# Moving the small product that turns the mu rows, in a retention and channel-mix kernel

## The chip, the cores and the metric

The kernel runs on one core of a Trainium2 chip. The metric is device time in microseconds (us) of one execution. PE is the matrix engine (TensorE) and PEld its weight loads, DVE the vector engine, ACT the scalar engine, POOL the engine that issues most input transfers, SP the one that issues the stores. An engine works through its own instructions in the order in which they were written, and waits at the first one whose inputs are not ready.

## What is computed

Two layers, one behind the other. The first is a linear attention with a decay gamma for each head (batch 4, 8 heads, 768 tokens, 64 features a head):

```python
for t in range(S):
    state = gamma * state + einsum('bhd,bhe->bhde', k[:, :, t], v[:, :, t])
    y[:, :, t] = scale * einsum('bhd,bhde->bhe', q[:, :, t], state)
x = y.transpose(0, 2, 1, 3).reshape(B, S, 512)
```

The second mixes each token with the one before it, by two vectors `mu_k` and `mu_r` of 512 numbers, and applies three weight matrices:

```python
xk = mu_k * x + (1 - mu_k) * x_prev
xr = mu_r * x + (1 - mu_r) * x_prev
k = maximum(xk @ w_k, 0)          # 512 -> 1024
v = k * k @ w_v                   # 1024 -> 512
out = sigmoid(xr @ w_r) * v
```

## The kernel before

The tokens are cut into 12 blocks of 256 (three for each batch entry). For a block, the attention runs in its chunked form. PE turns q and k (codes `Tq`, `Tk`, L272), ACT copies the turned halves out of PSUM (`Eq`, `Ek`, L241), PE makes the scores (`S`, L339 in block 0, L331 in blocks 1 to 5), DVE masks them (`M`, L354), DVE scales v (`vs`, L253), PE makes the block's addition to the state (`C`, L395 in block 0, L384 in block 1), DVE or ACT adds it up (`U`, L419 and L241), ACT applies the decay for the next block (`G`, L424), PE makes the output from masked scores and v (`Y`, L489 in block 0, L478 in block 1) and from the carried state (`I`, `J`, L441), and DVE writes it as x, token features across partitions (`D`, L514). `Y` of block 0 takes in the second part of the state's product too.

The second layer takes the difference of neighbouring tokens (`dx`, L529), mixes it with mu (`X`, L538), and runs the products `K` (L552, L562), `R` (L592) and `V` (L604), with Relu and Square on ACT (`Qa`, `Qb`), Sigmoid (`s`), the last multiplication on DVE (`O`, L610) and the store (`st`).

What sets the order is a string written out by hand, `ORDER` (L23 to L74). Each word is one step: a code, the block and further indices, `~` with an engine and `@` with the PSUM banks that it uses. L719 walks through the string and issues each step's instructions; so a word's place sets the place of its instructions in the queue of each engine. The scheduler adds semaphore waits where data or a PSUM bank demand them, and moves nothing.

Block 0 is done in two halves of the head pairs (`0.2` and `2.4` at the end of a word). Its first halves of q and k come through SP into a staging tile and are cast by ACT (`cq`, `ck`); the second halves come through POOL. Words `z.N` are products of a tile of zeros, N quarters of an fp32 product each (L667), or fp16 products for what is left of N by four (L674). Nobody reads their results.

The vectors mu come in as eight rows of 128 numbers: the word `mu` (L652) issues two transfers of 2 KB from ACT's queue. The word `mt` (`trans_mu`, L658) turns the eight rows on PE into eight columns, in PSUM bank 3. The word `me` (`copy_mu`, L661) copies these from PSUM to the tile `mu` on ACT. The first reader of that tile is the first `X` of block 0 on DVE. Behind `me` on ACT stand `gy.1` (L685, the upper half of a table of gamma powers, four instructions) and `G.0` (L424, four instructions).

Input tiles for q, k and v are rings of four, and POOL's transfers also take turns on eight completion semaphores: an issue waits for the one eight before it to land.

Of the kernel before, what the change touches and what calls it, by code (L numbers as in the profile page):

```python
# [20 lines left out]
WIDE = (1, 2, 3, 4, 5)  # L21
HEADS = ((0, 1), (3, 2), (4, 5), (7, 6))
ORDER = """  # L23
lk.0.0.2~s gy.0 lq.0.2.4~p lv.0~p lq.0.0.2~s lk.0.2.4~p ck.0.0.2~a z.12@6 Tk.0.0.2@0 mu Tq.0.2.4@1
cq.0.0.2~a z.2@6 Tq.0.0.2@2 Ek.0.0.2~a vs.0~v mt@3 Eq.0.0.2~a z.2@6 S.0.1.0.2@45 S.0.0.0.2@67
M.0.0.0.2~v Eq.0.2.4~a M.0.1.0.2~v Tk.0.2.4@2 Ek.0.2.4~a C.0@01 U.0.0~a U.0.1 S.0.0.2.4@67
M.0.0.2.4~v I.0@45 S.0.1.2.4@01 me M.0.1.2.4~v lv.1~p vs.1~v gy.1~a G.0~a z.4@2 Y.0 D.0~v lk.1~p
Tk.1@0 Ek.1~a C.1@67 U.1.0 lq.1~p z.1@2 Tq.1@1 Eq.1~a dx.0~v X.0.0.0 z.4@2 S.1.1@01 lk.2~p I.1@45
S.1.0@23 M.1.1~v M.1.0~v lq.2~p Tq.2@6 Eq.2~a wk.1~p X.0.0.3 Tk.2@0 X.0.0.2 z.1@1 Y.1 J.1 X.0.0.1
D.1~v U.1.1 Ek.2~a z.1@2 S.2.1@01 S.2.0@23 K.0.2@6 dx.1~v K.0.3@4 Qa.0.3 Qa.0.2 wk.0~p z.2@5  # L30
K.0.1@7 Qa.0.1 K.0.0@5 Qb.0.2 X.0.1.0 X.1.0.2 lv.2~p Qa.0.0 Qb.0.1 X.1.0.3 wr~p X.1.0.1 X.1.0.0
K.1.2@4 lv.3~p G.1~a K.1.1@7 X.0.1.1 vs.2~v Qa.1.2 Qb.1.2 M.2.1~v Qb.0.0 C.2@5 U.2.0 K.1.0@6
lq.3~p Qa.1.1 X.0.1.2 X.0.1.3 K.1.3@0 Qa.1.3 I.2@45 R.0.1@1 R.0.0@7 s.0.1 M.2.0~v Y.2 Qa.1.0
X.1.1.3 X.1.1.2 Qb.1.0 Tq.3@1 Eq.3~a J.2 X.1.1.0 X.1.1.1 R.1.0@6 s.0.0 lk.3~p Tk.3@1 vs.3~v D.2~v
dx.2~v X.2.0.2 X.2.0.0 C.3@23 X.2.0.3 Ek.3~a s.1.0 X.2.0.1 lk.4~p U.3.0~a R.1.1@0 lq.4~p s.1.1
Tk.4@1 S.3.1@45 S.3.0@67 Qb.1.1 Qb.1.3 U.3.1 lv.4~p Tq.4@0 Ek.4~a Eq.4~a wv.0~p K.2.2@2 Qa.2.2
M.3.1~v K.2.0@3 Qa.2.0 G.3~a M.3.0~v K.2.3@1 vs.4~v Qb.0.3 S.4.1@45 S.4.0@67 M.4.0~v I.3@23
M.4.1~v Qa.2.3 lq.6~p lq.7~p K.2.1@0 Qb.2.0 Y.3 C.4@67 V.1.0.0@1 U.4.0 U.4.1 G.4~a I.4@45 J.3
Qa.2.1 D.3~v dx.3~v Y.4 V.1.1.0@6 Tq.7@23 J.4 D.4~v wv.1~p Qb.2.1 V.0.1.0@0 lk.6~p V.0.0.0@7
X.2.1.2 dx.4~v X.3.0.1 X.3.0.2 X.3.0.3 Eq.7~a V.1.1.1 X.3.0.0 V.0.0.1 O.0.0 Tk.6@45 Ek.6~a lq.5~p  # L40
Tq.6@23 lv.5~p Qb.2.2 V.0.1.1 Eq.6~a V.1.0.1 O.1.0 K.3.6@4 K.3.1@5 Qb.2.3 lk.5~p K.3.0@7 Qa.3.6
Tq.5@4 Qa.3.1 Qa.3.0 vs.5~v C.5@5 X.2.1.1 Eq.5~a Tk.5@1 Ek.5~a S.6@23 O.0.1 O.1.1 lk.7~p U.5.0
Tk.7@67 Ek.7~a X.2.1.0 I.5@45 M.6~v X.3.1.3 K.3.2@0 K.3.3@1 Qa.3.2 Qb.3.1 lv.6~p S.5.0@23 Qa.3.3
Qb.3.0 X.3.1.1 S.5.1@67 Qb.3.3 X.2.1.3 Qb.3.2 K.3.4@0 st.0.0 Qa.3.4 M.5.1~v lk.8~p K.3.5@1 Qa.3.5
R.2.1@6 lv.8~p lk.9~p s.2.1 M.5.0~v Y.5 S.7@23 Tk.8@01 Ek.8~a J.5 X.3.1.0 X.3.1.2 R.3.1@7 s.3.1
V.2.0.0@6 K.3.7@0 lv.7~p vs.6~v R.2.0@7 V.2.0.1 D.5~v M.7~v s.2.0 dx.5~v X.5.1.1 O.2.0 Qa.3.7
Qb.3.6 V.2.1.0@1 Tk.9@23 C.6@45 U.6.0~a Ek.9~a lq.8~p Tq.8@67 Qb.3.7 X.5.0.3 V.2.1.1 vs.7~v
R.4.0@0 Eq.8~a U.6.1 U.6.2 X.5.0.0 U.6.3 st.0.1 R.3.0@2 C.7@45 X.5.0.1 s.4.0 I.6@67 s.3.0 st.1.1
X.5.0.2 K.5.3@3 Qa.5.3 O.2.1 lq.10~p K.5.1@0 Qa.5.1 G.6~v X.5.1.3 V.3.0.0@1 U.7.0 U.7.1 U.7.2
st.2.1 I.7@23 Y.6 vs.8~v U.7.3 G.7~a lq.11~p R.4.1@0 D.6~v V.4.1.0@4 lv.11~p C.8@67 Y.7 V.3.1.0@5  # L50
Qb.5.1 Qb.3.4 Qb.3.5 V.3.0.1 dx.6~v s.4.1 U.8.0 U.8.1 V.3.1.1 Qb.5.3 D.7~v U.8.2 V.4.1.1 dx.7~v
X.6.0.1 X.6.0.3 V.4.0.0@7 K.5.0@6 X.5.1.2 X.6.0.2 Qa.5.0 V.4.0.1 Qb.5.0 K.5.2@0 X.6.0.0 Qa.5.2
Qb.5.2 X.6.1.2 lv.9~p K.6.7@6 Qa.6.7 st.2.0 st.1.0 O.4.1 O.3.0 K.6.0@2 Qa.6.0 lk.10~p O.4.0 O.3.1
st.3.1 K.6.4@0 S.8@67 I.8@23 Tk.10@45 Qa.6.4 K.6.1@1 Ek.10~a X.6.1.1 X.5.1.0 Qa.6.1 Qb.6.1 K.6.6@0
Qb.6.0 Qa.6.6 vs.9~v K.6.5@4 Qa.6.5 M.8~v R.5.1@1 Qb.6.6 Tq.10@67 Eq.10~a s.5.1 Y.8 Tq.11@45
Qb.6.7 lv.10~p vs.10~v X.6.1.3 Eq.11~a D.8~v dx.8~v lq.9~p X.8.0.2 X.8.0.1 lk.11~p R.5.0@0 s.5.0
K.6.3@6 Qa.6.3 V.5.1.0@7 Tq.9@23 X.6.1.0 Eq.9~a S.10@45 M.10~v Qb.6.3 C.9@01 U.9.0~v st.3.0 U.9.1
V.5.1.1 K.6.2@6 Qa.6.2 R.6.1@2 s.6.1 U.9.2 R.6.0@3 s.6.0 I.9@45 U.9.3 O.5.1 X.8.0.3 S.9@01 M.9~v
X.8.0.0 G.9~a C.10@67 U.10.0 U.10.1 Qb.6.2 vs.11~v R.7.1@2 s.7.1 V.5.0.0@3 Qb.6.5 st.4.1 Tk.11@01
Ek.11~a U.10.2 U.10.3 V.5.0.1 Qb.6.4 K.8.0@2 Qa.8.0 G.10~v I.10@01 Y.9 C.11@67 st.4.0 R.7.0@2  # L60
O.5.0 V.6.1.0@3 D.9~v U.11.0 U.11.1 s.7.0 K.8.3@4 Qa.8.3 V.6.1.1 U.11.2 I.11@67 st.5.0 dx.9~v
O.6.1 S.11@45 X.8.1.2 Y.10 V.7.1.0@2 M.11~v D.10~v dx.10~v X.9.0.3 X.9.0.2 X.9.0.1 V.7.0.0@3 Y.11
X.9.0.0 Qb.8.0 K.8.2@4 Qa.8.2 X.8.1.0 X.9.1.1 K.8.1@5 Qa.8.1 D.11~v V.6.0.0@0 V.7.0.1 V.6.0.1
K.9.3@1 K.9.7@5 Qa.9.7 X.8.1.1 V.7.1.1 X.8.1.3 dx.11~v K.9.2@4 O.7.0 Qb.8.1 Qb.9.7 O.6.0 Qa.9.3
st.5.1 Qa.9.2 X.11.1.0 Qb.8.3 X.11.0.3 K.9.1@5 K.9.4@6 st.7.0 Qa.9.1 Qb.9.1 R.8.0@1 s.8.0
V.8.1.0@3 Qb.9.2 X.9.1.0 K.9.0@0 Qa.9.0 Qb.8.2 X.9.1.2 Qb.9.3 K.9.6@1 Qa.9.6 Qb.9.6 O.7.1 st.7.1
K.9.5@7 Qa.9.5 V.8.0.0@0 X.11.0.2 X.11.0.1 Qb.9.0 X.11.0.0 K.11.3@2 K.11.0@1 Qa.11.3 st.6.1
R.8.1@5 V.8.1.1 X.11.1.2 Qa.9.4 st.6.0 X.9.1.3 R.9.1@2 R.10.1@4 R.10.0@6 V.8.0.1 O.8.0 s.8.1
K.11.1@5 Qb.9.4 s.10.0 V.9.0.0@7 V.9.1.0@0 Qa.11.1 Qb.11.1 O.8.1 Qb.9.5 Qb.11.3 Qa.11.0 st.8.1
K.11.2@6 Qa.11.2 V.10.1.0@5 Qb.11.2 Qb.11.0 V.9.1.1 R.9.0@1 X.11.1.3 s.9.0 X.11.1.1 V.9.0.1 O.9.0  # L70
st.9.0 V.11.0.0@6 s.10.1 s.9.1 O.9.1 st.9.1 V.10.0.0@1 V.10.1.1 O.10.1 st.8.0 st.10.1 V.11.0.1
R.11.0@0 s.11.0 O.11.0 V.10.0.1 R.11.1@7 s.11.1 O.10.0 st.10.0 Vc.11.1.1@0 Oc.11.1.1 Vc.11.1.0@6
st.11.0 sc.11.1.1~a Oc.11.1.0 sc.11.1.0~s
"""  # L74


# [687 lines left out]
```

## Time and profile before

| | us |
|---|---|
| three runs | 158.83, 157.96, 158.57 |
| median of the runs | 158.57 |
| span of the profiled execution, first to last instruction | 158.7 |
| PE busy in it | 149.7 (94%) |
| DVE busy | 128.0 (81%) |
| ACT busy | 98.9 (62%) |
| POOL busy | 55.1 (35%) |

The span is what the profile gives as the profiled execution's own time; what lies around it is not told apart, and the median of the runs is within 0.2 us of it.

A share of busy time is a mean over stages with different limits. So the profile is read here by stretches: which engine is busy in which part of the span, which wait ended last, and what clock PE had (`PEclk`, 1.00 is full speed). In the timeline, a line gives the start in us, the duration in us, the engine, the line of the kernel, the operation with its tiles, the number of instructions merged, and in brackets the idle time ahead of it and what ended that.

### The profile page before, as it was taken

What the parts mean: (1) busy time and instruction counts of PE and PEld (TensorE: products, weight loads), DVE (VectorE), ACT (ScalarE), POOL (GpSimd) and SP (SyncE); (2) the same over time, 40 slices, a digit from 0 to 9 for tenths busy, and PEclk for the clock granted to TensorE, in tenths of its full rate; (3) what the DMA queues carried; (4) which work ended last, traced back from release to release, by engine and by line L of the source; (5) the groups of instructions that cost most, each with busy time, mean ns of one, the idle gap of its engine ahead of it and who ended that gap; (6) DMA issues with size and microseconds to landing.
All of it is one profiled execution on the core that took longest, in us unless ns stands there. A gap on an engine that the chain in (4) does not pass through costs nothing.

```text
span 158.7 us, 5316 instructions
## 1 busy us (share of the span) xinstructions
PE 149.7 (94%) x2316; PEld 85.5 (54%) x2316; DVE 128.0 (81%) x203; ACT 98.9 (62%) x182; POOL 55.1 (35%) x67
## 2 busy tenths in 40 slices
PE   7749989999999999999999999999999999999992
PEld 3334667765765445545654555555565445555451
DVE  2258799999999999999999999999999998040432
ACT  3437452989967479947662689978313498529330
POOL 7999426827967507702992000000000000000000
PEclk9985799999999999999999999999999999999998
DMA  5999999999999999990799934000300015001335
GB/s 151 273 181 175 203 244 243 162 238 182 182 201 179 218 215 175 192 171 9 170 316 216 98 121 150 4 6 0 136 6 4 0 66 197 1 0 70 130 135 198
DMA packets 44903, 22.29 MB, mean 140 GB/s; under 512 B 36424, under 2 KB 40400, under 8 KB 44880
## 3 DMA queue, kind: packets, MB, share of 16 engines
q0 software_dynamic: 39920, 14.95, 73.6%
q1 hardware_dynamic: 4512, 6.69, 11.7%
q10 hardware_dynamic: 448, 0.32, 0.7%
q8 instruction: 18, 0.29, 0.7%
q14 instruction: 5, 0.04, 0.1%
HBM read 24.31 MB, written 6.29 MB: 193 GB/s over the span
## 4 chain that ended last, share of the span: by engine, by line
PE 48%; DVE 31%; DMA 9%; issue 6%; ACT 4%; POOL 0%; DVEq 0%; POOLq 0%
PE ps L604 13%; PE ps L552 9%; PE ps L592 8%; DVE a L354 5%; PE ps L562 5%; DVE xk L538 4%; DVE xr L538 4%; DMA k<-in_k_dram 3%; DVE dx L529 3%; DMA mu<-in_moe_mu_r_dram 3%; DVE vs L253 3%; DVE tg L419 2%; DVE os L610 2%; DVE xT L507 2%; DMA k2s<-in_k_dram 2%
## 5 line engine op out<-in xcount | busy, mean ns | idle before, releaser
L604 PE MATMUL ps<-wv,k2s 128*128 128x512 f16 x184 | 44.4, 380 | 0.0
L571 ACT ACTIVATE kr<-ps 128x512 f32<-128x512 f32 x48 | 27.8, 597 | 21.6 <-PE ps L562 14.6
L604 PEld LDWEIGHTS <-k2s 128*128 128x128 f16 x184 | 17.3, 98 | 18.8
L610 DVE SCALAR_TENSOR_TENSOR os<-ps,rs 128x512 f32<-128x512 f32 x23 | 15.1, 685 | 14.4 <-PE ps L604 7.9
L592 PE MATMUL ps<-wr,xr 128*128 128x512 f16 x96 | 23.9, 380 | 0.0
L230 POOL DMA_DIRECT2D k<-in_k_dram x22 | 19.7, 915 | 12.1 <-PE ps L318 6.6
L562 PE MATMUL ps<-xk,wk 128*128 128x256 f16 x192 | 23.6, 273 | 0.2 <-DVE xk L538 0.2
L552 PE MATMUL ps<-xk,wk 128*128 128x512 f16 x96 | 22.6, 380 | 0.8 <-DVE xk L538 0.8
L598 ACT ACTIVATE rs<-ps 128x512 f32<-128x512 f32 x24 | 14.1, 602 | 13.9 <-PE ps L592 9.8
L230 POOL DMA_DIRECT2D v<-in_v_dram x22 | 19.8, 919 | 8.4 <-DVE vs L253 7.9
L562 PEld LDWEIGHTS <-wk 128*128 128x128 f16 x192 | 18.2, 98 | 4.8 <-DVE xk L538 0.5
L538 DVE SCALAR_TENSOR_TENSOR xr<-dx,mu,xT 128x256 f16<-128x256 f32 (+1 forms) x36 | 19.4, 569 | 0.0
L538 DVE SCALAR_TENSOR_TENSOR xk<-dx,mu,xT 128x256 f16<-128x256 f32 (+1 forms) x36 | 18.8, 568 | 0.2
L241 ACT COPY kT<-ps 128x1024 f16<-128x1024 f16 (+1 forms) x13 | 12.2, 951 | 9.3 <-PE ps L272 5.9
L253 DVE TENSOR_TENSOR vs<-v,csm_sb 128x1024 f16<-128x1024 f32 x12 | 14.6, 1219 | 3.1 <-DMA v<-in_v_dram 3.1
L354 DVE TENSOR_TENSOR a<-ps,c_sb 128x1024 f16<-128x1024 f32 (+1 forms) x14 | 14.4, 1067 | 1.9 <-PE ps L339 1.5
L552 PEld LDWEIGHTS <-wk 128*128 128x128 f16 x96 | 9.0, 98 | 12.1 <-DVE xk L538 1.1
L583 ACT ACTIVATE k2s<-kr 128x512 f16<-128x512 f32 x24 | 14.8, 632 | 0.2
L529 DVE TENSOR_TENSOR dx<-xT 128x1024 f32<-128x1024 f32 x12 | 14.7, 1222 | 0.2
L579 ACT ACTIVATE k2s<-kr 128x512 f16<-128x512 f32 x24 | 14.7, 628 | 0.1
L241 ACT COPY qT<-ps 128x1024 f16<-128x1024 f16 (+1 forms) x13 | 12.3, 952 | 3.5 <-PE ps L272 3.4
L592 PEld LDWEIGHTS <-xr 128*128 128x128 f16 x96 | 8.7, 98 | 9.7
(67 smaller groups left out, 157.8 us busy)
## 6 DMA issues: line engine op xcount, KB each, us to landing
out_dram<-os SPq DMA_DIRECT2D x23, 256.0 KB, 2.4
v<-in_v_dram POOLq DMA_DIRECT2D x22, 256.0 KB, 7.2
k<-in_k_dram POOLq DMA_DIRECT2D x23, 128.0 KB, 7.0
q<-in_q_dram POOLq DMA_DIRECT2D x11, 256.0 KB, 7.7
wk<-in_moe_w_k_dram POOLq DMA_DIRECT2D x2, 512.0 KB, 10.9
wv<-in_moe_w_v_dram POOLq DMA_DIRECT2D x2, 512.0 KB, 8.0
v<-in_v_dram POOLq DMA_DIRECT2D x1, 512.0 KB, 6.2
wr<-in_moe_w_r_dram POOLq DMA_DIRECT2D x1, 512.0 KB, 13.2
```

The source lines that it names most:

```text
L230: e.dma_start(out=dst[:, :, i * D : i * D + D], in_=src[:, i * P : i * P + P].rearrange("h p d -> p h d"),)
L241: e.copy(out=out, in_=in_)
L253: e.tensor_tensor(out=VS(n), in0=V32(n).rearrange("p h (i d) -> p i h d", i=2), in1=gks[:, int(half(n) or wide(n)), :, :, None].to_broadca ...
L354: nc.vector.tensor_tensor(out=a_full(n)[:, i, :, j0:j1], in0=pairs(banks("S", n, i, j0))[:, :, j0:j1], in1=(below if wide(n) else causal[: ...
L529: e.tensor_tensor(out=DX(k)[:, :, m * TM + t0 : m * TM + t1], in0=x[:, :, c + t0 : c + t1], in1=x[:, :, c - 1 + t0 : c - 1 + t1], op=ALU.s ...
L538: nc.vector.scalar_tensor_tensor(out=XM[w](k)[:, j, t0:t1], in0=DX(k)[:, j, t0:t1], scalar=mu[:, w * NCO + j : w * NCO + j + 1], in1=x[:, ...
L552: nc.tensor.matmul(banks("K", n, g), lhsT=wk16[:, co, g * P : g * P + P], rhs=XM[0](k)[:, co, :], start=(co == 0), stop=(co == NCO - 1),)
L562: nc.tensor.matmul(pz[:, i, :], lhsT=wk16[:, co, fo * P : fo * P + P], rhs=XM[0](k)[:, co, m * TM + t0 : m * TM + t1], start=(i == 0 and c ...
L571: nc.scalar.activation(out=kr, in_=banks("K", n, g, *u), func=AF.Relu)
L592: nc.tensor.matmul(banks("R", n, tb), lhsT=XM[1](k)[:, co, t : t + P], rhs=wr16[:, co, :], start=(co == 0), stop=(co == NCO - 1),)
L604: nc.tensor.matmul(banks("V", n, tb), lhsT=K2(n)[:, fo, tb * P : tb * P + P], rhs=wv16[:, fo, :], start=(fo == 0), stop=(fo == NFO - 1),)
L610: nc.vector.scalar_tensor_tensor(out=OS(2 * n + tb), in0=banks("V", n, tb), scalar=1.0 / (KSC * KSC), in1=RS(2 * n + tb), op0=ALU.mult, op ...
```

## The change

One word of `ORDER` changes its place. `mt@3` stood behind `vs.0~v`, ahead of the second pair of zero products and of the first scores of block 0. It now stands behind `S.0.1.2.4@01`, the last scores of block 0, and directly ahead of `me`. The string is wrapped anew, so that it takes one line more and later lines of the kernel count one higher; its other 629 words stand in the same order.

```diff
-... mu Tq.0.2.4@1 cq.0.0.2~a z.2@6 Tq.0.0.2@2 Ek.0.0.2~a vs.0~v mt@3 Eq.0.0.2~a z.2@6
+... mu Tq.0.2.4@1 cq.0.0.2~a z.2@6 Tq.0.0.2@2 Ek.0.0.2~a vs.0~v Eq.0.0.2~a z.2@6
 S.0.1.0.2@45 S.0.0.0.2@67 M.0.0.0.2~v Eq.0.2.4~a M.0.1.0.2~v Tk.0.2.4@2 Ek.0.2.4~a
 C.0@01 U.0.0~a U.0.1 S.0.0.2.4@67
-M.0.0.2.4~v I.0@45 S.0.1.2.4@01 me M.0.1.2.4~v lv.1~p vs.1~v gy.1~a G.0~a z.4@2 Y.0 D.0~v
+M.0.0.2.4~v I.0@45 S.0.1.2.4@01 mt@3 me M.0.1.2.4~v lv.1~p vs.1~v gy.1~a G.0~a z.4@2 Y.0 D.0~v
```

On PE, the one product of L659 goes from ahead of the zero products to between the last scores and the next zero product. On ACT, the order is the same, and the copy of mu (L662) gets a wait for PE that the instruction ahead of it covered before. The queues of DVE, POOL and SP hold the same instructions in the same order with the same waits.

More of the change, by code (lines that the diff above doesn't have):

```diff
@@ L23 @@
 ORDER = """
[L24 to L71, printed above, removed]
@@ L72 @@
-R.11.0@0 s.11.0 O.11.0 V.10.0.1 R.11.1@7 s.11.1 O.10.0 st.10.0 Vc.11.1.1@0 Oc.11.1.1 Vc.11.1.0@6
-st.11.0 sc.11.1.1~a Oc.11.1.0 sc.11.1.0~s
+lk.0.0.2~s gy.0 lq.0.2.4~p lv.0~p lq.0.0.2~s lk.0.2.4~p ck.0.0.2~a z.12@6 Tk.0.0.2@0 mu
+Tq.0.2.4@1 cq.0.0.2~a z.2@6 Tq.0.0.2@2 Ek.0.0.2~a vs.0~v Eq.0.0.2~a z.2@6 S.0.1.0.2@45
+S.0.0.0.2@67 M.0.0.0.2~v Eq.0.2.4~a M.0.1.0.2~v Tk.0.2.4@2 Ek.0.2.4~a C.0@01 U.0.0~a U.0.1
+S.0.0.2.4@67 M.0.0.2.4~v I.0@45 S.0.1.2.4@01 mt@3 me M.0.1.2.4~v lv.1~p vs.1~v gy.1~a G.0~a
@@ new lines @@
+z.4@2 Y.0 D.0~v lk.1~p Tk.1@0 Ek.1~a C.1@67 U.1.0 lq.1~p z.1@2 Tq.1@1 Eq.1~a dx.0~v X.0.0.0
+z.4@2 S.1.1@01 lk.2~p I.1@45 S.1.0@23 M.1.1~v M.1.0~v lq.2~p Tq.2@6 Eq.2~a wk.1~p X.0.0.3 Tk.2@0
+X.0.0.2 z.1@1 Y.1 J.1 X.0.0.1 D.1~v U.1.1 Ek.2~a z.1@2 S.2.1@01 S.2.0@23 K.0.2@6 dx.1~v K.0.3@4
+Qa.0.3 Qa.0.2 wk.0~p z.2@5 K.0.1@7 Qa.0.1 K.0.0@5 Qb.0.2 X.0.1.0 X.1.0.2 lv.2~p Qa.0.0 Qb.0.1
+X.1.0.3 wr~p X.1.0.1 X.1.0.0 K.1.2@4 lv.3~p G.1~a K.1.1@7 X.0.1.1 vs.2~v Qa.1.2 Qb.1.2 M.2.1~v
+Qb.0.0 C.2@5 U.2.0 K.1.0@6 lq.3~p Qa.1.1 X.0.1.2 X.0.1.3 K.1.3@0 Qa.1.3 I.2@45 R.0.1@1 R.0.0@7
@@ new lines @@
+s.0.1 M.2.0~v Y.2 Qa.1.0 X.1.1.3 X.1.1.2 Qb.1.0 Tq.3@1 Eq.3~a J.2 X.1.1.0 X.1.1.1 R.1.0@6 s.0.0
+lk.3~p Tk.3@1 vs.3~v D.2~v dx.2~v X.2.0.2 X.2.0.0 C.3@23 X.2.0.3 Ek.3~a s.1.0 X.2.0.1 lk.4~p
+U.3.0~a R.1.1@0 lq.4~p s.1.1 Tk.4@1 S.3.1@45 S.3.0@67 Qb.1.1 Qb.1.3 U.3.1 lv.4~p Tq.4@0 Ek.4~a
+Eq.4~a wv.0~p K.2.2@2 Qa.2.2 M.3.1~v K.2.0@3 Qa.2.0 G.3~a M.3.0~v K.2.3@1 vs.4~v Qb.0.3 S.4.1@45
+S.4.0@67 M.4.0~v I.3@23 M.4.1~v Qa.2.3 lq.6~p lq.7~p K.2.1@0 Qb.2.0 Y.3 C.4@67 V.1.0.0@1 U.4.0
+U.4.1 G.4~a I.4@45 J.3 Qa.2.1 D.3~v dx.3~v Y.4 V.1.1.0@6 Tq.7@23 J.4 D.4~v wv.1~p Qb.2.1
@@ new lines @@
+V.0.1.0@0 lk.6~p V.0.0.0@7 X.2.1.2 dx.4~v X.3.0.1 X.3.0.2 X.3.0.3 Eq.7~a V.1.1.1 X.3.0.0 V.0.0.1
+O.0.0 Tk.6@45 Ek.6~a lq.5~p Tq.6@23 lv.5~p Qb.2.2 V.0.1.1 Eq.6~a V.1.0.1 O.1.0 K.3.6@4 K.3.1@5
+Qb.2.3 lk.5~p K.3.0@7 Qa.3.6 Tq.5@4 Qa.3.1 Qa.3.0 vs.5~v C.5@5 X.2.1.1 Eq.5~a Tk.5@1 Ek.5~a
+S.6@23 O.0.1 O.1.1 lk.7~p U.5.0 Tk.7@67 Ek.7~a X.2.1.0 I.5@45 M.6~v X.3.1.3 K.3.2@0 K.3.3@1
+Qa.3.2 Qb.3.1 lv.6~p S.5.0@23 Qa.3.3 Qb.3.0 X.3.1.1 S.5.1@67 Qb.3.3 X.2.1.3 Qb.3.2 K.3.4@0
+st.0.0 Qa.3.4 M.5.1~v lk.8~p K.3.5@1 Qa.3.5 R.2.1@6 lv.8~p lk.9~p s.2.1 M.5.0~v Y.5 S.7@23
@@ new lines @@
+Tk.8@01 Ek.8~a J.5 X.3.1.0 X.3.1.2 R.3.1@7 s.3.1 V.2.0.0@6 K.3.7@0 lv.7~p vs.6~v R.2.0@7 V.2.0.1
+D.5~v M.7~v s.2.0 dx.5~v X.5.1.1 O.2.0 Qa.3.7 Qb.3.6 V.2.1.0@1 Tk.9@23 C.6@45 U.6.0~a Ek.9~a
+lq.8~p Tq.8@67 Qb.3.7 X.5.0.3 V.2.1.1 vs.7~v R.4.0@0 Eq.8~a U.6.1 U.6.2 X.5.0.0 U.6.3 st.0.1
+R.3.0@2 C.7@45 X.5.0.1 s.4.0 I.6@67 s.3.0 st.1.1 X.5.0.2 K.5.3@3 Qa.5.3 O.2.1 lq.10~p K.5.1@0
+Qa.5.1 G.6~v X.5.1.3 V.3.0.0@1 U.7.0 U.7.1 U.7.2 st.2.1 I.7@23 Y.6 vs.8~v U.7.3 G.7~a lq.11~p
+R.4.1@0 D.6~v V.4.1.0@4 lv.11~p C.8@67 Y.7 V.3.1.0@5 Qb.5.1 Qb.3.4 Qb.3.5 V.3.0.1 dx.6~v s.4.1
@@ new lines @@
+U.8.0 U.8.1 V.3.1.1 Qb.5.3 D.7~v U.8.2 V.4.1.1 dx.7~v X.6.0.1 X.6.0.3 V.4.0.0@7 K.5.0@6 X.5.1.2
+X.6.0.2 Qa.5.0 V.4.0.1 Qb.5.0 K.5.2@0 X.6.0.0 Qa.5.2 Qb.5.2 X.6.1.2 lv.9~p K.6.7@6 Qa.6.7 st.2.0
+st.1.0 O.4.1 O.3.0 K.6.0@2 Qa.6.0 lk.10~p O.4.0 O.3.1 st.3.1 K.6.4@0 S.8@67 I.8@23 Tk.10@45
+Qa.6.4 K.6.1@1 Ek.10~a X.6.1.1 X.5.1.0 Qa.6.1 Qb.6.1 K.6.6@0 Qb.6.0 Qa.6.6 vs.9~v K.6.5@4 Qa.6.5
+M.8~v R.5.1@1 Qb.6.6 Tq.10@67 Eq.10~a s.5.1 Y.8 Tq.11@45 Qb.6.7 lv.10~p vs.10~v X.6.1.3 Eq.11~a
+D.8~v dx.8~v lq.9~p X.8.0.2 X.8.0.1 lk.11~p R.5.0@0 s.5.0 K.6.3@6 Qa.6.3 V.5.1.0@7 Tq.9@23
@@ new lines @@
+X.6.1.0 Eq.9~a S.10@45 M.10~v Qb.6.3 C.9@01 U.9.0~v st.3.0 U.9.1 V.5.1.1 K.6.2@6 Qa.6.2 R.6.1@2
+s.6.1 U.9.2 R.6.0@3 s.6.0 I.9@45 U.9.3 O.5.1 X.8.0.3 S.9@01 M.9~v X.8.0.0 G.9~a C.10@67 U.10.0
+U.10.1 Qb.6.2 vs.11~v R.7.1@2 s.7.1 V.5.0.0@3 Qb.6.5 st.4.1 Tk.11@01 Ek.11~a U.10.2 U.10.3
+V.5.0.1 Qb.6.4 K.8.0@2 Qa.8.0 G.10~v I.10@01 Y.9 C.11@67 st.4.0 R.7.0@2 O.5.0 V.6.1.0@3 D.9~v
+U.11.0 U.11.1 s.7.0 K.8.3@4 Qa.8.3 V.6.1.1 U.11.2 I.11@67 st.5.0 dx.9~v O.6.1 S.11@45 X.8.1.2
+Y.10 V.7.1.0@2 M.11~v D.10~v dx.10~v X.9.0.3 X.9.0.2 X.9.0.1 V.7.0.0@3 Y.11 X.9.0.0 Qb.8.0
@@ new lines @@
+K.8.2@4 Qa.8.2 X.8.1.0 X.9.1.1 K.8.1@5 Qa.8.1 D.11~v V.6.0.0@0 V.7.0.1 V.6.0.1 K.9.3@1 K.9.7@5
+Qa.9.7 X.8.1.1 V.7.1.1 X.8.1.3 dx.11~v K.9.2@4 O.7.0 Qb.8.1 Qb.9.7 O.6.0 Qa.9.3 st.5.1 Qa.9.2
+X.11.1.0 Qb.8.3 X.11.0.3 K.9.1@5 K.9.4@6 st.7.0 Qa.9.1 Qb.9.1 R.8.0@1 s.8.0 V.8.1.0@3 Qb.9.2
+X.9.1.0 K.9.0@0 Qa.9.0 Qb.8.2 X.9.1.2 Qb.9.3 K.9.6@1 Qa.9.6 Qb.9.6 O.7.1 st.7.1 K.9.5@7 Qa.9.5
+V.8.0.0@0 X.11.0.2 X.11.0.1 Qb.9.0 X.11.0.0 K.11.3@2 K.11.0@1 Qa.11.3 st.6.1 R.8.1@5 V.8.1.1
+X.11.1.2 Qa.9.4 st.6.0 X.9.1.3 R.9.1@2 R.10.1@4 R.10.0@6 V.8.0.1 O.8.0 s.8.1 K.11.1@5 Qb.9.4
@@ L74 @@
+s.10.0 V.9.0.0@7 V.9.1.0@0 Qa.11.1 Qb.11.1 O.8.1 Qb.9.5 Qb.11.3 Qa.11.0 st.8.1 K.11.2@6 Qa.11.2
+V.10.1.0@5 Qb.11.2 Qb.11.0 V.9.1.1 R.9.0@1 X.11.1.3 s.9.0 X.11.1.1 V.9.0.1 O.9.0 st.9.0
+V.11.0.0@6 s.10.1 s.9.1 O.9.1 st.9.1 V.10.0.0@1 V.10.1.1 O.10.1 st.8.0 st.10.1 V.11.0.1 R.11.0@0
+s.11.0 O.11.0 V.10.0.1 R.11.1@7 s.11.1 O.10.0 st.10.0 Vc.11.1.1@0 Oc.11.1.1 Vc.11.1.0@6 st.11.0
+sc.11.1.1~a Oc.11.1.0 sc.11.1.0~s
 """
```

## Prediction

> **What bounds the kernel now.** I read the page by slices first, to see which engine is full where.
>
> ```profile
> PE   7749989999999999999999999999999999999992
> DVE  2258799999999999999999999999999998040432
> PEclk9985799999999999999999999999999999999998
> ```
>
> A slice is 4 us. From the sixth slice on PE and DVE are both full; until then neither is, and PE's clock falls to half in the fourth slice. The busy times by stretch put numbers to that: from 20.54 to 124.00 DVE is busy 101.22 of 103.46 us, and from there PE carries the rest to the end. So a start of the full stretch that comes earlier by some time moves the end by the same, as long as no transfer holds it back. The question is the first 20 us.
>
> Second, the chain of work that ended last, in order of time:
>
> ```profile
> 4.58 5.20 DMA mu<-in_moe_mu_r_dram
> 9.79 0.14 issue
> 9.92 0.20 PE ps L659
> 10.12 0.54 PE ps L674 x2
> 10.65 0.35 PE ps L339 x16
> 11.00 0.54 PE ps L272 x8
> ...
> 12.98 0.46 PE ps L339 x8
> 13.44 2.00 PE ps L667 x2
> 15.45 1.00 PE ps L489 x29
> 16.44 0.21 PE ps L441 x4
> 16.66 1.00 PE ps L272 x16
> 17.65 0.38 PE ps L384 x16
> 18.03 0.32 PE ps L674
> 18.36 0.59 PE ps L272 x16
> ```
>
> The transfer of the mu rows is on the path that sets the end: 5.20 us to land, and PE stands at L659 until 9.79. Nothing behind L659 needs mu for another ten us (the first mixing is at 19.71).
>
> Third, the timeline, for what else was ready:
>
> ```profile
> 7.87 1.07 ACT L241 COPY qT<-ps 128x512 f16<-128x512 f16 x2 [1.47 <-PE ps L272]
> 8.31 1.22 DVE L253 TENSOR_TENSOR vs<-v,csm_sb 128x1024 f16<-128x1024 f32 x1 [3.09 <-DMA v<-in_v_dram]
> 9.92 0.20 PE L659 MATMUL ps<-csm_sb,mu 8*128 8x8 f32 x1 [2.09 <-DMA mu<-in_moe_mu_r_dram]
> 11.05 1.29 DVE L354 TENSOR_TENSOR a<-ps,c_sb 128x512 f16<-128x512 f32 x2 [1.52 <-PE ps L339]
> ```
>
> PE idles 2.09 us (7.83 to 9.92); DVE idles 1.52 us for the scores. The first half of the turned q is there at about 8.41 (half of the two copies from 7.87), the turned k at 6.4.
>
> Last, PE by stretches of 3.4 us (columns: length, busy time and count of PE, PEld, DVE, ACT, POOL, then PE's clock, DMA share, GB/s):
>
> ```profile
> 4.19:7.60 3.41, 2.66 (x27) 0.99 (x27) 0.94 (x3) 1.60 (x3) 3.41 (x5) 1.00 1.34 270
> 7.60:11.02 3.42, 1.33 (x31) 0.66 (x29) 1.22 (x1) 1.07 (x2) 3.42 (x5) 1.00 1.61 192
> 11.02:14.43 3.41, 3.31 (x62) 1.92 (x62) 3.18 (x6) 2.87 (x11) 3.29 (x5) 0.50 2.15 167
> 14.43:17.85 3.42, 3.42 (x70) 2.31 (x68) 1.97 (x2) 0.43 (x3) 2.33 (x3) 0.50 1.54 197
> ```
>
> The clock is half from 11.02 to 17.85, right behind the stretch in which PE was busy only 1.33 of 3.42 us.
>
> **The change, part by part.** *The wait goes.* The zero pair (0.60 us) runs at 7.83, the first scores at 8.46 when the copy of qT is done, and end by 8.9 (16 in 0.42 us). The second half of k was issued at 3.01 and took 5.9 us, so its turning (8 products) starts at 8.9 too. What is late next is DVE: `vs.0` ends at 9.53, whatever PE does. Then two masks (1.29) to 10.82 and the sum `U.0.1` (0.42) to 11.24, against 12.96 before. `C.0` needs `vs.0` and runs 9.55 to about 9.9; the next copy of kT is done at about 9.9, `U.0.0` at 10.3, so neither holds up DVE. The last scores share their banks with `C.0` and wait for `U.0.1`, so they start at 11.26, against 12.98: **1.72 us earlier**.
>
> *The product's new place.* It finds mu landed at 9.78, with nothing to wait for. Its 0.20 us now stands behind the last scores on the path: minus 0.20, so **1.5 us** at the following zero product. Bounds for the 0.20: nothing, if it hides under the wait of `Y.0` for the last mask, and 0.40 at half clock. That mask ends at 11.24 + 1.29 = 12.53; the zero product takes 2.00 at half clock or 1.12 at full (the row at 18.85), so it ends after the mask. I take 0.20.
>
> *The copy of mu* now waits for this product, at about 11.9 instead of running at 12.41: earlier. Behind it on ACT stand `gy.1` (1.28) and `G.0` (1.05), which end near 14.3; before, they ended at 14.70. The readers are `D.0`, which comes at 13.7 at the earliest and needs only `gy.1` (13.3), and `U.1.0` behind it. So the wait costs nothing; if the product came 0.4 us later than I have it, `D.0` would begin to feel it.
>
> *The clock.* If the half clock stays where it was, Y.0 ends 1.5 us earlier, but then `Tq.1` (0.59 at full clock, 1.00 as for the same count in `Tk.1` at half) falls inside it. That takes 0.4 back: **1.1 us** left. If the clock stays up at 11.02, the rows at half clock shorten: zeros 2.00 to 1.12; L489 1.00 to some 0.70 (an estimate: 16 scores took 0.35 at full clock); L441 0.21 to 0.12; the turning 1.00 to 0.59; `C.1` 0.38 to 0.30. Sum 1.76, with the 1.5 some 3.2.
>
> *What the transfers allow.* They depend on one another, not on this change, until 30 us. Issue plus time to landing against use: v of block 1 lands at 11.25, `vs.1` ran at 14.09 (slack 2.8); q of block 2 at 18.15, turned at 20.92 (2.8); the halves of w_k at 20.7 and 23.3, used at 24.62 and 26.81 (3.9 and 3.5); later loads have 4 and more. So a shift up to 2.8 us passes and one of 3.2 may lose 0.4. From 36.65 on POOL waits for buffers that compute frees, and moves with it.
>
> Is the clock kept? PE's busy time from 7.60 to 11.02 becomes, by the rows above: end of the turning 0.23, zeros 0.60, scores 0.42, turning of k 0.41, `C.0` 0.35, scores 0.25, `I.0` 0.2: about 2.4 of 3.42 us. The stretch with 1.33 was followed by half clock, the one with 2.66 was not; 2.4 is nearer to 2.66. I take the clock as kept, and of 2.8 to 3.2 I take 2.4, since the second cap is close and each later wait for a landing gives back a little. Against the span: 158.7 - 2.4 = **156.3 us**. The median of the runs is 0.13 below the span, less than their spread of 0.87, so I leave it at that. Own range of this case: 155.4 to 157.0.
>
> The trace shows the clock falling after a wait of 2.09 us in a stretch of 3.42. [...]
>
> **The rivals.**
>
> 1. *The clock falls all the same.* [...] Gain 1.1 us: 157.6; 157.2 if the half-clock stretch moves forward with the work.
>
> 2. *The time is absorbed.* A load that I hold to have slack lands later, or a stretch of PE between 30 and 90 us is the real bound. For it: PE is as full there as DVE. Against: the order is fixed, so PE's stretch shifts as well. 158.1 to 158.7.
>
> 3. *Slower: the half clock lasts longer.* It falls at 11.02 and is not lifted at 17.85. The stretch 11.02 to 14.43 was 3.31 of 3.41 busy and did not lift it, so busy time alone doesn't; with the work 1.1 us earlier, 14.43 to 17.85 holds turning and other small products in other shares. If it stays half for another 3.4 us, the products until 21.3 (`Tq.1`, zeros of 1.12, scores, turnings of block 2) take some 1.8 us more: 158.7 - 1.1 + 1.8 = 159.4. The point from which it decides is an added half-clock time of 2 us.
>
> That the change doesn't do what it says has no room: PE's queue shows the one product behind the last scores.
>
> **How the numbers follow.** Forecast 45%, rival 1 27%, rival 2 15%, rival 3 13%. The range reaches from the forecast's lower end, 155.4, up through rivals 1 and 2 to 158.8; it leaves out rival 3 and a little on the other side. A measurement of this kernel tells about 0.5% (0.8 us) from no change: faster means below 157.8. Forecast and most of rival 1 are there: 0.70; same 0.17, with rival 2 and the rest of rival 1; slower 0.13.
>
> **What would show it.** Right: L659 at about 11.6 with no wait; the first mask at 9.53 directly behind `vs.0`; the last scores at 11.26; clock 1.00 at 11.02 to 14.43; `D.0` near 13.7 instead of 16.76 and the masks of block 1 near 17.7 instead of 20.54. Rival 1 has `D.0` at 15.3 and these masks at 19.5 with clock 0.50 in between. Rival 2 has them early, and a new DVE or PE wait for a load later. Rival 3 has clock 0.50 beyond 17.85. I am wrong in the base if the first mask does not move, that is, if the scores waited for something besides PE's queue.

## The result, and the profile after

The changed kernel takes 156.24 us (156.09 to 156.53, four runs) where the kernel before takes 158.70 us (157.96 to 160.46, four runs). The ratio to the kernel before is 0.988, with a 95% interval of 0.9837 to 0.9923. The forecast was 156.3. The comparison takes executions within 1.5% of the fastest of their kernel, which leaves out most executions of the kernel before in which PE's clock fell for 6.8 us; where I say that an execution kept its clock, its mean clock is 0.995 or more.

The profiled execution of the changed kernel took 156.10 us, with a span of 154.3: 1.8 us lie outside the span. So they do in every execution that was listed with both numbers, to 0.1 us. The profiled execution of the kernel before, with its span of 158.7, therefore was the one of 160.46 us, not one like the median of 158.57 with which I had set it equal.

The page by slices, after:

```profile
PE   7979899999999999999999999999998999999991
DVE  2499999989999999999999999999999996050531
PEclk9999999999999999999999999999999999999999
```

DVE is full from the third slice on instead of the sixth, and the clock has no dip. The timeline of the changed kernel around the old and the new place:

```profile
7.76 1.22 DVE L254 TENSOR_TENSOR vs<-v,csm_sb 128x1024 f16<-128x1024 f32 x1 [2.10 <-DMA v<-in_v_dram]
8.90 1.28 DVE L355 TENSOR_TENSOR a<-ps,c_sb 128x512 f16<-128x512 f32 x2
...
10.35 0.52 PE L340 MATMUL ps<-qT,kT 64*64 64x128 f16 x8
...
10.80 0.22 PE L660 MATMUL ps<-csm_sb,mu 8*128 8x8 f32 x1
10.95 1.12 PE L668 MATMUL ps<-zero 128*128 128x512 f32 x2
11.06 0.17 ACT L663 COPY mu<-ps 128x8 f32<-128x8 f32 x1 [1.14 <-PE ps L660]
...
11.63 1.21 DVE L254 TENSOR_TENSOR vs<-v,csm_sb 128x1024 f16<-128x1024 f32 x1
12.01 0.64 PE L490 MATMUL ps<-a,vs 64*64 64x128 f16 x32
...
12.86 1.23 DVE L515 TENSOR_TENSOR xT<-ps,gy_sb 128x1024 f32<-128x1024 f32 x1
...
16.08 2.36 DVE L355 TENSOR_TENSOR a<-ps,c_sb 128x1024 f16<-128x1024 f32 x2
...
17.24 0.64 PE L273 MATMUL ps<-c_sb,q 128*64 128x128 f16 x16 [0.70 <-DMA q<-in_q_dram]
```

Two rows of the kernel before to set beside it, its last scores of block 0 and its masks of block 1:

```profile
12.78 0.66 PE L339 MATMUL ps<-qT,kT 64*64 64x128 f16 x8
...
20.54 2.36 DVE L354 TENSOR_TENSOR a<-ps,c_sb 128x1024 f16<-128x1024 f32 x2 [0.34 <-PE ps L331]
```

The product of mu (now L660) waits for nothing. The first mask follows the scaling of v without a gap; before, DVE stood 1.52 us there. The zero product takes 1.12 us instead of 2.00 and the output product of block 0 0.64 instead of 1.00, with PE's clock at 1.00 instead of 0.50. The masks of block 1 start at 16.08 instead of 20.54, 4.46 us earlier; the span is 4.4 us shorter. What the first 16 us gain arrives at the end in full. Some of it is chance: by the start of its scaling, v of block 0 landed at 7.76 here, at 8.31 in the profile before, and between 7.75 and 8.96 in all the profiles of this case. In the changed kernel DVE's work follows that landing without a gap, so with 8.31 the gain would have been some 0.55 us smaller (an estimate).

PE by stretches of the changed kernel (same columns as before):

```profile
7.60:11.02 3.42, 2.60 (x80) 1.92 (x78) 3.26 (x5) 1.81 (x4) 3.42 (x5) 1.00 1.61 194
11.02:14.43 3.41, 3.41 (x89) 2.20 (x88) 3.39 (x6) 3.32 (x10) 3.41 (x5) 1.00 2.13 168
```

PE is busy 2.60 us where it was busy 1.33, and the clock stays at 1.00.

### The profile page after: what moved, and what is told of

It is laid out like the page before. It is cut to its first block, busy times and chain, and to the rows that moved or that the text cites. A ratio compares the mean times of both kernels' runs of the same rounds, so it can differ in the third digit from the quotient of the medians.

```text
span 154.3 us, 5316 instructions
## 1 busy us (share of the span) xinstructions
PE 147.3 (95%) x2316; PEld 84.2 (55%) x2316; DVE 128.1 (83%) x203; ACT 99.1 (64%) x182; POOL 55.2 (36%) x67
## 4 chain that ended last, share of the span: by engine, by line
PE 42%; DVE 36%; issue 8%; POOL 6%; DMA 5%; ACT 3%; DVEq 0%; POOLq 0%
PE ps L605 13%; PE ps L553 9%; PE ps L593 8%; DVE xk L539 6%; PE ps L563 5%; DVE dx L530 5%; DMA q<-in_q_dram 5%; DVE xr L539 4%; DVE a L355 4%; DVE xT L515 3%; DVE vs L254 3%; DVE tg L420 3%; DVE os L611 2%; POOL k L231 2%; DVE xT L508 2%
## 5 line engine op out<-in xcount | busy, mean ns | idle before, releaser
(67 smaller groups left out, 154.3 us busy)
## 6 DMA issues: line engine op xcount, KB each, us to landing
wk<-in_moe_w_k_dram POOLq DMA_DIRECT2D x2, 512.0 KB, 10.2
```

## The experiments

A gain of 4.4 us from profile to profile is more than twice the 2.09 us of the wait. My theory after the result: there are two costs, a wait in every execution and a fall of the clock behind it in some. The rivals: the clock's fall is the whole of it, or the cost is the place of the product and not its wait. The experiments ran on several chips; in each, executions of the kernel before ran on the same chip beside them.

**Both kernels again.** No edit.

> The kernel before, unchanged, to see each execution's span and mean clock beside its time. Theory 1 (two costs: a wait of PE for mu in every execution, and a fall of PE's clock behind it in only some of them): the times fall into two groups some 2 us apart, about 158.3 with a mean clock near 1.00 and about 160.4 with a mean clock near 0.976. Theory 2 (the fall of the clock belongs to the wait and comes in every execution): all executions have a mean clock near 0.976, and times within 0.9 us of 158.6. Time less span should be 1.8 us as in the kernel after.

> The changed kernel, unchanged. Theory 1 and theory 2 both expect mean clocks of 0.997 to 1.00 and times of 156.1 to 156.6. [...]

The kernel before falls into groups. In this run and the executions of the same kernel beside it, 13 executions kept their clock, at 157.68 to 158.05 us; one at 159.48 had a mean clock of 0.989; 20 stood at 160.05 to 161.24 with 0.977 to 0.979; eight at 161.65 to 161.90 with 0.967 or 0.968. Since half clock for t us of the span lowers the mean by t/2 over the span, these are some 3.4, 7 and 10 us at half clock (an estimate; the profiles of this case show 3.41 us in an execution with 0.989 and 6.83 us in two with 0.976 and 0.978). The stretches of a second profile of the kernel before, cut at its own changes of clock:

```profile
8.54:11.95 3.41, 1.80 (x59) 1.09 (x59) 1.43 (x3) 0.53 (x2) 3.41 (x5) 1.00 1.80 172
11.95:15.36 3.41, 3.30 (x32) 1.47 (x35) 3.12 (x5) 2.51 (x11) 3.41 (x5) 0.50 2.13 168
```

The fall comes at 11.95 here, at 11.02 in the first profile, and lasts 6.83 us in both: the place in the kernel at which it comes differs between these two executions.

The changed kernel kept its clock in 8 of 12 executions (156.32 to 156.92, median 156.40) and had 0.989 in four (157.58 to 158.73). So theory 2 is out, since the fall is not in every execution before. Theory 1 was off too: after the change the fall is rarer (4 of 12 executions, against 29 of 42 before) and shorter (0.989, against mostly 0.977 to 0.979), but not gone: that the changed kernel keeps its clock is in part chance. With the clock kept in both, on the same chip, the change is worth 157.77 - 156.40 = **1.4 us**. Against the group of 20 (median 160.4) it is worth 4.0 us. Over all executions the medians on this chip are 160.3 (42 executions) and 156.66 (12).

**The wait filled with zero products.**

```diff
-vs.0~v mt@3 Eq.0.0.2~a
+vs.0~v z.8@6 mt@3 Eq.0.0.2~a
```

> The kernel before with eight more zero quarters (two fp32 products, some 2.2 us) ahead of the waiting product, so that PE is busy through the wait for mu. It keeps the wait and takes away the idle time. If the clock is most of the gain (theory 2), this alone gives 156.5 to 157.5 although the wait stands. If the wait itself is most of the gain (theory 1), time stays within 0.5 us of the executions of the kernel before that kept their clock, about 158.3, and the clock is 1.00 in all of them.

It took 157.81 us (157.54 to 158.20), and all 12 executions kept their clock (0.997 to 1.00). Its profile, one stretch and then the timeline:

```profile
7.60:11.02 3.42, 3.19 (x33) 1.38 (x31) 1.34 (x2) 1.07 (x2) 3.42 (x5) 1.00 1.60 194
```

```profile
9.78 0.20 PE L659 MATMUL ps<-csm_sb,mu 8*128 8x8 f32 x1 [0.23 <-DMA mu<-in_moe_mu_r_dram]
10.91 1.29 DVE L354 TENSOR_TENSOR a<-ps,c_sb 128x512 f16<-128x512 f32 x2 [1.82 <-PE ps L339]
```

The product still runs at 9.78 when mu lands, and DVE still waits 1.82 us for the scores; yet the clock stays. The time is that of the kernel before where it kept its clock (157.77), so the 1.4 us above are the wait, or the product's place. So the two costs come apart: with the idle time filled (PE busy 3.19 us of 3.42, against 1.33 in the first profile) the clock was kept in 12 of 12 executions, against 13 of 42 of the kernel before on the same chip, and the 1.4 us are left.

**The product in its old place, its data earlier.**

```diff
-lq.0.0.2~s lk.0.2.4~p ck.0.0.2~a z.12@6 Tk.0.0.2@0 mu Tq.0.2.4@1
+lq.0.0.2~s mu lk.0.2.4~p ck.0.0.2~a z.12@6 Tk.0.0.2@0 Tq.0.2.4@1
...
-            nc.scalar.dma_start(
+            nc.sync.dma_start(
                 out=mu8[w * NCO : (w + 1) * NCO], in_=x.rearrange("(co ci) -> co ci", ci=P)
```

> The kernel before with the product in its old place, and the two transfers of mu issued from SP's queue right behind the first halves of k and q (about 1.8 us into the span) instead of from ACT at 4.0 us. It takes the wait away and leaves the place. If the wait was the cost, it lands before 7.8 us and this gives what the changed kernel gives, 156.0 to 156.8. If the place was the cost (a product between turning and scores, with its own weight load, and the copy of mu behind it), it stays at 158 to 158.6.

It took 156.21 us (156.10 to 157.09, six executions, all with 0.997 or more), ratio to the kernel before 0.9859 (0.9779 to 0.9939). The profile is of the slowest of the six, in which v landed late, at 8.96:

```profile
8.12 0.22 PE L659 MATMUL ps<-csm_sb,mu 8*128 8x8 f32 x1
...
8.96 1.23 DVE L253 TENSOR_TENSOR vs<-v,csm_sb 128x1024 f16<-128x1024 f32 x1 [3.80 <-DMA v<-in_v_dram]
10.11 1.28 DVE L354 TENSOR_TENSOR a<-ps,c_sb 128x512 f16<-128x512 f32 x2
```

In the old place and with no wait, the product costs nothing that shows: DVE again goes from the scaling of v to the mask without a gap. On the same chip, it is 156.21 against 156.40 for the changed kernel, both with the clock kept. It was the wait, not the place.

**The wait filled with transposes.** As with the zero products, but with a word `tz.32@6` that issues 32 transposes of the identity.

```diff
+    def turns(e, count):
+        pz = banks("tz", count).bitcast(F16)
+        for x in range(count):
+            nc.tensor.transpose(pz[:, x % 8 * P : x % 8 * P + P], ident, ident)
...
-vs.0~v mt@3 Eq.0.0.2~a
+vs.0~v tz.32@6 mt@3 Eq.0.0.2~a
```

> The kernel before with 32 transposes of the identity (128x128 fp16, some 2 us in all) ahead of the waiting product, where the run with zero products had two fp32 products. The wait stays. If transposes hold up PE's clock as products do (theory: PE's busy time decides), it is as with the zero products: 157.5 to 158.2 with mean clock 0.997 to 1.00 in all executions. [...]

All 12 executions kept their clock (0.996 to 1.00). In its profile the 32 transposes take 1.96 us from 7.48 on, PE is busy 3.22 of 3.42 us from 7.60 to 11.02, and the clock stays at 1.00: they hold it up here as the zero products did, where the kernel before kept it in 4 of 23 executions on the same chip. The time was not as expected, though: 159.14 us (158.56 to 159.38), where the kernel before with its clock kept took 157.65 on the same chip (median of four). The profile, of an execution of 158.58, shows this on PE:

```profile
15.58 0.47 PE L272 MATMUL ps<-c_sb,q 128*64 128x128 f16 x9
16.66 0.41 PE L272 MATMUL ps<-c_sb,q 128*64 128x128 f16 x7 [0.61 <-issue]
```

The masks of block 1, first in the run with zero products and then in this one:

```profile
17.97 2.36 DVE L354 TENSOR_TENSOR a<-ps,c_sb 128x1024 f16<-128x1024 f32 x2
18.68 2.35 DVE L354 TENSOR_TENSOR a<-ps,c_sb 128x1024 f16<-128x1024 f32 x2 [0.81 <-PE ps L331]
```

In the middle of one turning PE stops for 0.61 us with nothing that it waited for in the profile ("issue"), and the masks come 0.71 us later. That covers the 0.65 us between the two profiled executions (158.58 and 157.93, on different chips). Why PE stops there, and what the slower executions of this run lose besides, stays open.

**The zero products around the turning taken out.** In the changed kernel, without the two words `z.2@6` of block 0 ahead of its scores.

> The changed kernel without the two pairs of fp16 zero products around the turning of block 0 (1.2 us of PE between 6.4 and 7.9 us). DVE starts the first mask when v is scaled, so the time of PE's products is not on the path. If the new idle time lets the clock fall, most executions have a mean clock near 0.978 and 157.5 to 159; if the moved product's wait was the only thing that let it fall, the clock is kept as in the changed kernel and the time is 156.2 to 156.5.

Three of 12 executions kept the clock (156.19 to 156.41), seven had 0.985 to 0.989 and two 0.975 (up to 159.42); the median is 157.64. With the clock kept the time is that of the changed kernel, so these 1.2 us of PE are off the path. The clock was kept in 3 of 12 executions without them and in 12 of 16 of the changed kernel with them. These were not on one chip, but the counts point to the products helping to hold up the clock. Most falls were again the shorter kind (0.989), not the 0.978 expected.

**The product further back.**

```diff
-S.0.1.2.4@01 mt@3 me M.0.1.2.4~v lv.1~p vs.1~v gy.1~a G.0~a z.4@2 Y.0 D.0~v
+S.0.1.2.4@01 M.0.1.2.4~v lv.1~p vs.1~v gy.1~a G.0~a z.4@2 Y.0 mt@3 me D.0~v
```

> The changed kernel with the product of mu moved on once more, behind the output product of block 0, and the copy of mu behind the decay on ACT. My prediction charged 0.20 us for the product on the path: then this gains 0.1 to 0.2 us, 156.2. The other theory is that DVE (second masks, scaling of v of block 1, output of block 0 without a gap) sets the time there: then nothing changes, 156.4 within 0.1.

It took 155.98 us (155.73 to 157.50, six executions), ratio to the kernel before 0.9843 (0.9757 to 0.9928). At the place in question nothing was gained: the output of block 0 started at 12.78 against 12.86, and the masks of block 1 at 16.10 against 16.08, as the theory of DVE has it. Its span is 0.3 us shorter all the same, and the profiles part much later, at the output of block 2: there the changed kernel has 0.35 us of idle DVE (start at 32.40), this one none (31.98). I don't know what ties that to the edit, and the changed kernel itself was not run on this chip (the three executions above with the clock kept, 156.19 to 156.41, are the nearest to it there), so the 0.3 us is not shown to be the edit's.

**v of block 0 loaded first.**

```diff
-gy.0 lq.0.2.4~p lv.0~p lq.0.0.2~s
+gy.0 lv.0~p lq.0.2.4~p lq.0.0.2~s
...
-Tq.0.2.4@1 cq.0.0.2~a z.2@6 Tq.0.0.2@2
+cq.0.0.2~a Tq.0.0.2@2 z.2@6 Tq.0.2.4@1
```

> The changed kernel with the load of v of block 0 issued ahead of the second half of q, and the first half of q turned ahead of the second. If the landing of v is now what the first mask waits for (theory: the scaling of v, then DVE without a gap), v lands some 0.8 us earlier and the time falls by 0.4 to 0.8 us, to 155.6 to 156.0. If something else bounds it by then (scores, the copy of turned q), it stays at 156.4.

Slower than the changed kernel, not faster: 156.85 us (156.39 to 157.32). v landed at 7.80, no earlier than behind q (7.76 in the changed kernel), and the half of q landed at 8.51 (in the changed kernel PE turned it at 6.07), so that PE and with it the first mask (9.86) came late. Here the other order of issue on POOL's queue delayed the one load by 2.4 us or more and did not bring the other forward.

**More filling in the changed kernel.** One zero product `z.1@3` behind the turning of the second half of k; or three, `z.3@7`, ahead of the turning of q of block 2; or both, with the product further back. In the two kernels with `z.3@7`, these products overwrite the second half of block 1's addition to the state before it is added, so that part is missing from the output; no other work is left out.

> The changed kernel with one more fp16 zero product behind the turning of the second half of k, where PE waits about 0.3 us for v to be scaled. In 4 of 12 executions of the changed kernel the mean clock was 0.989, one stretch of half clock of some 3.4 us. If the short idle times between 8.7 and 11 us let the clock fall there, this raises the least mean clock to 0.997 or more in all executions, and none is above 157.0. If the fall comes later (while PE waits for q of block 2 at 16.5 to 17.2 us), about a third still have 0.989. DVE sets the time at this place, so executions with a kept clock stay at 156.2 to 156.5.

> The changed kernel with three more fp16 zero products ahead of the turning of q of block 2, where PE waits 0.7 us for that load. If this wait, together with the products' short idle times from 14.4 to 17.8 us, lets the clock fall in a third of the executions, all of them now have a mean clock of 0.997 or more. If the fall comes from the stretch before 11 us, about a third still have 0.989. Executions with a kept clock stay at 156.2 to 156.5; up to 0.2 us more if the three products outlast the wait.

> Both fillings, and the product of mu behind the output product of block 0 as in the run that moved it on once more. Expected to have a kept clock in all executions and 155.9 to 156.3, below both kernels, if the later place is worth the 0.2 to 0.3 us that it showed; 156.4 if that was a difference between chips.

The first: 12 of 13 executions kept the clock, 156.20 to 157.00, and one had 0.989 (158.45). The second: 9 of 12 kept it (median 156.66), three had 0.985 to 0.989. Both: 10 of 11 kept it (median 156.03, from 155.80), one had 0.989. Against 8 of 12 without filling, none of these counts is far enough off to name the stretch that lets the clock fall; the question is undecided. Nor do the times say what a filling costs: on this chip the kernel before with its clock kept took 157.13 (median of eight), 0.6 less than on the first chip, and the changed kernel without filling was not run there. The profile of the first caught such a fall, cut at its changes of clock:

```profile
8.51:11.92 3.41, 2.67 (x80) 1.89 (x80) 3.30 (x6) 1.54 (x5) 3.28 (x5) 1.00 1.84 173
11.92:15.33 3.41, 3.41 (x46) 1.74 (x48) 1.99 (x4) 2.30 (x9) 3.13 (x5) 0.50 2.12 170
```

It falls behind a stretch with 2.67 us of 3.41 busy, and stays 3.41 us. In the first profile of the kernel before, the stretch from 4.19 to 7.60 held 2.66 us, and the clock stayed up behind it.

**The same in a free bank**, `z.3@6`, with the whole computation:

> The changed kernel with both fillings and the later place of the product, the second filling now in bank 6, where the products of the block before have been read. Whole computation. Against the run with the second filling in bank 7 only the bank differs, so 155.8 to 156.3 with a kept clock in nearly all executions, 0.8 to 1.2% below the kernel before where that kept its clock; were the gain of the later place a difference between chips, 156.2 to 156.5.

It took 156.33 us (156.02 to 156.84, six executions, all with 0.996 or more), ratio to the kernel before 0.9883 (0.9832 to 0.9935). It is no faster than the changed kernel on the first chip (156.40) beyond their spread, and six executions are too few to call its clock safe.

## Why the prediction came out right, point by point

The direction and the mechanism held; that the number agrees so well is luck, because two terms were off against each other.

- *What bounds the kernel.* Right in the main. But I read PE as not full before the sixth slice, and its row has 9 in the fourth and fifth, where it works at half clock (0.50 from 11.02 to 17.85).
- *The wait for mu is on the path and goes.* Right: no wait at L660, and 1.4 us with the clock kept in both kernels. I had 1.5 for the wait and the new place.
- *What is late next is the scaling of v.* Right: the mask follows it without a gap, at 8.90. I had 9.53, for v landed at 7.76 in this execution and not at 8.31.
- *The last scores come 1.72 us earlier.* Mis-sized against the profile: the timeline has them at 10.35, and before at 12.78: 2.4 us earlier. Of the 0.7 us that I missed, 0.55 is the earlier landing of v, which is no effect of the change. The rest is that DVE's instructions here start some 0.08 us before the listed end of the one ahead (8.90 against 7.76 + 1.22, and at the sum 10.10 against 8.90 + 1.28); I had set them end to end.
- *The product's 0.20 us on the path.* Not borne out. The output of block 0 starts behind DVE's own work at 12.84, and moving the product on changed that start by 0.08 and the masks of block 1 not at all.
- *The copy of mu and what stands behind it.* Right: 11.06, `G.0` ends at 13.37, and nobody waits.
- *The clock is kept.* Right in the profile and in 12 of 16 executions of the changed kernel; in the other four it fell for some 3.4 us (an estimate from their mean clock of 0.989), which cost 157.74 - 156.40 = 1.3 us. My reason for it was weak, and that it held is partly luck: I set PE's busy time, 2.4 us (measured 2.60), beside 2.66 that kept the clock and 1.33 that did not, and in another run the clock fell behind 2.67.
- *Of 2.8 to 3.2 us I took 2.4.* This term was mis-sized: from profile to profile it was 4.4. I cut it for the landing of q of block 2, and PE did wait 0.70 us for it (until 17.24; I had it landing at 18.15), but DVE worked on its masks until 18.4 (16.08 and 2.36) and lost nothing. My sum also went along PE's rows, while in the changed kernel DVE works without a gap from 7.76 on and sets the time; and some 0.55 of the 4.4 is the landing of v. The rows at half clock shortened as worked out (2.00 to 1.12; 1.00 to 0.64, estimated 0.70).
- *The span stands for the time of the median run.* This step was wrong. The profiled execution of before took 160.46 us, 1.9 above the median, with 1.8 us outside its span. Taking 2.4 off a span gave 156.3; right would have been 4.4 off 160.46, which is 156.1. The two errors (1.8 and 2.0) cancel by chance. The 2.46 us between the two measured medians are no single effect either: the four executions before lie between 157.96 and 160.46, so their median mixes kept and fallen clocks, and the 2.46 lies between the 1.4 and the 4.0 us of the groups.
- *Rival 1, the clock falls all the same.* Its outcome happens in a minority of executions: in four of 16, at 157.58 to 158.73. Whether 2.4 us of busy PE is too little stays open: the 2.60 of the profile kept the clock, and in another run it fell behind 2.67.
- *Rival 2, absorbed.* No: the gain is 4.46 us at the masks of block 1 and 4.4 at the end.
- *Rival 3, a longer half clock.* Not in the changed kernel. In the kernel before it is there: the executions at 161.65 and more have some 10 us of it, an estimate from their mean clock (0.967 or 0.968).

## What to carry to other kernels

A small product whose data came late held up the products queued behind it on PE here: PE stood 2.09 us at it, and the time was 1.4 us longer. Issue the load of such a product earlier, or put it where its data have landed; here both gave the same (156.21 and 156.40). Where an engine falls idle in the same place, ask for the clock as a cost of its own, and test it by filling the idle time with work that nobody reads: here that took away 2.6 us (160.4 to 157.8) and left the 1.4 us of the wait. And list time, span and mean clock of many executions before a profile's span is set equal to a median.

## What the runs showed of the hardware

- Half clock lasted 3.41 us in the profile of the run with one filling and 6.83 us, twice that, in two profiles of the kernel before; by the mean clock of 0.967 or 0.968 it lasted some 10.2 us, three times that, in the slowest group of the kernel before (an estimate). It began at 11.02 in one of the two profiles of that kernel and at 11.95 in the other. The falls followed 3.4 us with 1.33, 1.80 and even 2.67 us of busy PE.
- The clock was kept behind a stretch with less work and fell behind one with more. In the second profile of the kernel before, the stretch from 5.13 to 8.54 held 2.22 us of busy PE, and the clock stayed at 1.00 for the next 3.41 us, until 11.95; in the run with one filling it fell behind 2.67 us. Both stretches are cut by whole lengths of 3.41 us back from the change of the clock:

```profile
5.13:8.54 3.41, 2.22 (x28) 0.84 (x26) 1.18 (x3) 2.28 (x4) 3.41 (x5) 1.00 1.27 280
```

So busy time over these stretches, as the profile counts it (2.22 kept, 2.67 fallen), does not decide alone. What does is not shown by these runs.
